# Output products with 17 weight columns, batch rows 16 partitions apart, and one output transfer of eight partitions in place of two of four

## The chip, the cores and the metric

One core of one Trainium2 chip. The time is device microseconds of one execution; lower is better. Each number of a run is the median of its executions. The execution's time is mostly 1.7 to 2.1 us longer than the span of its instructions, which the profile shows; both are given where it matters. Executions of one kernel on one chip mostly lie within 0.3%, so differences below that need several rounds, and their intervals are given.

## The reference, cut to what matters

One decoding step for two rows (B = 2): layernorm, attention with a window of 2048 of the cached keys and values for 16 key heads, its output product with `wo`, and beside it a squared-ReLU MLP, all added to the input.

```python
W = min(4096, max(256, Sk // 4))                 # 2048
k = k_cache[:, :, Sk - W:, :];  v = v_cache[:, :, Sk - W:, :]
o = softmax(q @ k.T * Dh ** -0.5) @ v             # per head
attention = o.reshape(B, 1, Hq * Dh) @ wo         # 4096 x 576
mlp = relu(xn @ w1 + b1) ** 2 @ w2 + b2           # 576 x 4608, 4608 x 576
return x + attention + mlp                        # (2, 1, 576), bf16
```

The core must read 53.6 MB and computes little on them.

## The kernel before

K and V of a unit (four heads of one batch row) are 2 MB each and go through one pool of six buffers of 16384 bytes in each partition; the weights of `wq`/`w1` and `wo` have pools of their own. All pools lie one behind the other in SBUF, after a pool `const` of small things, in this order:

```python
const  = ctx.enter_context(tc.tile_pool(name="const", bufs=1))
kvpool = ctx.enter_context(tc.tile_pool(name="kvpool", bufs=6))       # K, V, most of w2
ktpool = ctx.enter_context(tc.tile_pool(name="ktpool", bufs=6))       # K transposed: engines only
wbig   = ctx.enter_context(tc.tile_pool(name="wbig", bufs=NFULL // RW))   # wq, w1, the rest of w2
wrem   = ctx.enter_context(tc.tile_pool(name="wrem", bufs=2))
wopool = ctx.enter_context(tc.tile_pool(name="wopool", bufs=1))       # wo
...
def issue_kv(tiles, cache, u, name, parts=1):
    tl = kvpool.tile([P, UE], BF16, tag="kv", name=f"{name}_{u}")
    ...   # nc.sync.dma_start(out=tl[...], in_=v[...])
```

All products that end in the output have two weight columns (the two batch rows). Most go to `out_ps`, each with the two halves of the 576 columns in two column groups of TensorE; the last part of `w2`, which arrives last, goes to `tail_ps` in four groups of 144 columns:

```python
ones_b = const.tile([1, B], BF16, name="ones_b")
def out_acc(lhsT, rhs_of, start=False, stop=False, pin=False):
    for i in range(2):
        mm = nc.tensor.matmul(out_ps[32 * i:32 * i + B, :], lhsT=lhsT, rhs=rhs_of(i * OH, (i + 1) * OH), ...)
...
for i in range(4):
    cp = nc.scalar.copy if i % 2 else nc.vector.tensor_copy
    cp(out=part[32 * i:32 * i + B, :], in_=out_ps[32 * (i // 2):32 * (i // 2) + B, (i % 2) * OQ:(i % 2 + 1) * OQ])
for w in W2P[NG4 - 1:]:
    mlp_tail(*w[1:])                              # tail_ps, four groups
fin_sb = work.tile([RB, OQ], BF16, tag="fin", name="fin_sb")
nc.vector.tensor_tensor(out=fin_sb[:], in0=mlp["out"][0:RB, :], in1=part[:], op=ALU.add)
for b, eng in ((0, nc.sync), (1, nc.scalar)):
    eng.dma_start(out=out2d[b:b + 1, :].rearrange("o (q n) -> (o q) n", q=4), in_=fin_sb[b:RB:32, :])
```

So batch row b of quarter q lies in partition 32q + b, and each batch row leaves in a transfer of its own.

Of the kernel before, what the change touches and what calls it, by code (L numbers as in the profile page):

```python
# [8 lines left out]
F32 = mybir.dt.float32  # L9
BF16 = mybir.dt.bfloat16  # L10
ACT = mybir.ActivationFunctionType
ALU = mybir.AluOpType
# [4 lines left out]
def kernel(  # L17
# [14 lines left out]
    nc = tc.nc  # L32
    P = 128
    B, Sq, D = A_x.shape
# [27 lines left out]
    NG4 = 4  # L62
# [5 lines left out]
    FR = HW // P  # L68
# [7 lines left out]
    N3 = (NG4 - 1) * FR  # L76
    NFC = N3 + len(CX)
    RB = 32 * (NG4 - 1) + B
    OH = D // 2
    OQ = D // 4  # L80
    NP = NQ // 2
    WR = 2 * NC * Dh // P
# [3 lines left out]
    const = ctx.enter_context(tc.tile_pool(name="const", bufs=1))  # L86
    kvpool = ctx.enter_context(tc.tile_pool(name="kvpool", bufs=6))
    ktpool = ctx.enter_context(tc.tile_pool(name="ktpool", bufs=6))
    wbig = ctx.enter_context(tc.tile_pool(name="wbig", bufs=NFULL // RW))
    wrem = ctx.enter_context(tc.tile_pool(name="wrem", bufs=2))  # L90
    wopool = ctx.enter_context(tc.tile_pool(name="wopool", bufs=1))
    work = ctx.enter_context(tc.tile_pool(name="work", bufs=2))
    keep = ctx.enter_context(tc.tile_pool(name="keep", bufs=3))
    psum = ctx.enter_context(tc.tile_pool(name="psum", bufs=1, space=bass.MemoryType.PSUM))

    x2d = A_x.rearrange("b s d -> (b s) d")
    out2d = out.rearrange("b s d -> (b s) d")
# [74 lines left out]
    x_sb = const.tile([B, D], BF16, name="x_sb")  # L172
# [20 lines left out]
                                    scalar1=float(32 * q))  # L193
    ident = const.tile([P, P], BF16, name="ident")
    nc.vector.tensor_scalar(out=ident[:], in0=col_f[:], scalar1=row_f[:, 0:1], scalar2=None, op0=ALU.is_equal)
    ones_b = const.tile([1, B], BF16, name="ones_b")
    nc.vector.memset(ones_b[:], 1.0)

    half_d = D // 2
    stats = const.tile([B, 2, 6], F32, name="stats")  # L200
# [34 lines left out]
    with nc.allow_low_precision(reason="sums of one 1 and zeros"):  # L235
        nc.vector.tensor_reduce(out=rmask[:], in_=ident[:].rearrange("p (c r) -> p r c", r=WR), axis=AX.X, op=ALU.add)
        nc.vector.tensor_reduce(out=sel[:, MZ:MZ + DW], in_=ident[:].rearrange("p (c r) -> p c r", r=WR), axis=AX.X,
                                op=ALU.add)

    out_ps = psum.tile([32 + B, OH], F32, tag="out", name="out_ps")  # L240
    nc.vector.memset(out_ps[:], 0.0)

    def out_acc(lhsT, rhs_of, start=False, stop=False, pin=False):
        for i in range(2):
            mm = nc.tensor.matmul(out_ps[32 * i:32 * i + B, :], lhsT=lhsT, rhs=rhs_of(i * OH, (i + 1) * OH),  # L245
                                  start=start, stop=stop, skip_group_check=True)
            if pin:
                tc.keep_in_program_order(mm)
# [7 lines left out]
    def q_block(c):  # L256
# [6 lines left out]
        if c == KC - 1:  # L263
            qrow = const.tile([RB, QW], BF16, tag="row", name="qrow")
            nc.vector.tensor_copy(out=qrow[:, 0:QB], in_=q_ps[0][0:RB, :])  # L265
            nc.scalar.copy(out=qrow[:, QB:QW], in_=q_ps[1][0:RB, :])
            qT_ps = psum.tile([P, QH, P], BF16, tag="sc", bufs=2, name="qT_ps")
            for i in range(QH):
                nc.tensor.transpose(out=qT_ps[:, i, 0:RB], in_=qrow[:, i * Dh:(i + 1) * Dh],
                                    identity=ident[0:RB, 0:RB])  # L270
            qT_v = qT_ps[:].rearrange("p i (g s) -> p i g s", s=32)
# [68 lines left out]
            pT_tiles.pop(u)  # L340

    wo_state = {}

    def wo_sel(t):
        rr = work.tile([P, WR, 2 * NC * B], BF16, tag="rr", bufs=1, name=f"rr_{t}")
        for i in range(2):
            oG = oG_tiles.pop(2 * t + i)
            nc.vector.tensor_tensor(
                out=rr[:, :, i * NC * B:(i + 1) * NC * B],
                in0=oG[:].rearrange("p h b -> p (h b)").unsqueeze(1).to_broadcast([P, WR, NC * B]),  # L350
                in1=rmask[:].unsqueeze(2).to_broadcast([P, WR, NC * B]), op=ALU.mult)
        wps = psum.tile([P, WR, B], F32, tag="misc", bufs=2, name=f"wps_{t}")
        for h in range(2 * NC):
            nc.tensor.matmul(wps[:], lhsT=sel[:, MZ - h * DW:MZ - h * DW + P],
                             rhs=rr[:, :, h * B:(h + 1) * B], start=(h == 0), stop=(h == 2 * NC - 1))
        ws = work.tile([P, WR, B], BF16, tag="ws", name=f"ws_{t}")
        nc.vector.tensor_copy(out=ws[:], in_=wps[:])  # L357
        wo_state[t] = ws

    def wo_acc(tq):  # L360
        ws = wo_state.pop(tq)
        wo_sb = wo_tiles.pop(tq)
        for r in range(WR):
            out_acc(ws[:, r, :], lambda a, z: wo_sb[:, r, a:z])

    mlp = {}
# [15 lines left out]
    def mlp_h_end():  # L382
        hrow = const.tile([RB, HW], BF16, tag="row", name="hrow")
        for k in range(3):
            t1_t = work.tile([P, NJ, NC], F32, tag="sub", name=f"t1_{k}")
            t1 = t1_t[:].rearrange("p j c -> p (j c)")[0:RB, 0:HB]
            nc.scalar.activation(out=t1, in_=mlp["ps"][k][0:RB, :], func=ACT.Relu)
            nc.vector.tensor_tensor(out=hrow[:, k * HB:(k + 1) * HB], in0=t1, in1=t1, op=ALU.mult)
        hT_sb = const.tile([P, NFC, B], BF16, name="hT_sb")
        ha = psum.tile([P, FR, 96], BF16, tag="sc", bufs=2, name="ha_ps")  # L390
        hb = psum.tile([P, len(CX), B], BF16, tag="sc", bufs=2, name="hb_ps")
        ra = 32 * (NG4 - 2) + B
        for r in range(FR):
            nc.tensor.transpose(out=ha[:, r, 0:ra], in_=hrow[0:ra, r:HW:FR], identity=ident[0:ra, 0:ra])
        rb = 32 * (NG4 - 1)
        for i, (c0, st, m) in enumerate(CX):
            nc.tensor.transpose(out=hb[0:m, i, :], in_=hrow[rb:RB, c0:c0 + (m - 1) * st + 1:st],
                                identity=ident[rb:RB, rb:RB])
        ha_v = ha[:].rearrange("p r (g s) -> p g r s", s=32)
        for b in range(B):  # L400
            nc.vector.tensor_copy(out=hT_sb[:, 0:N3, b].rearrange("p (g r) -> p g r", r=FR), in_=ha_v[:, :, :, b])
        for i0, i1, m in ((0, FT, P), (FT, FT + XR, XP), (FT + XR, len(CX), XQ)):
            nc.vector.tensor_copy(out=hT_sb[0:m, N3 + i0:N3 + i1, :], in_=hb[0:m, i0:i1, :])
        mlp["h"] = hT_sb

    def mlp_o(g, r0, r1):
        w2_sb = w2_tiles.pop((g, r0))
        for r in range(r0, r1):
            o = (r - r0) * D
            out_acc(mlp["h"][:, g * FR + r, :], lambda a, z: w2_sb[:, o + a:o + z], stop=(g == NG4 - 2 and r == r1 - 1))  # L410

    part = const.tile([RB, OQ], F32, name="part")
    nc.gpsimd.memset(part[:], 0.0)

    def mlp_tail(r0, r1):
        w2_sb = w2_tiles.pop((NG4 - 1, r0))
        if r0 == 0:
            mlp["out"] = psum.tile([P, OQ], F32, tag="misc", bufs=2, name="tail_ps")
            nc.vector.memset(mlp["out"][:], 0.0)
        for r in range(r0, r1):  # L420
            o = (r - r0) * D
            for i in range(4):
                nc.tensor.matmul(mlp["out"][32 * i:32 * i + B, :], lhsT=mlp["h"][:, (NG4 - 1) * FR + r, :],
                                 rhs=w2_sb[:, o + i * OQ:o + (i + 1) * OQ], start=(r == 0), stop=(r == FT - 1),
                                 skip_group_check=True, tile_position=(0, 32 * i))

# [5 lines left out]
    def load_k(u):  # L432
        for f in issue_kv(k_tiles, A_k_cache, u, "k"):
            f()
        if u >= 3:
            issue_w2x()
# [31 lines left out]
    for g in range(NG):  # L468
# [7 lines left out]
                          in_=ident[0:NG4, 0:NG4].unsqueeze(2).to_broadcast([NG4, NG4, 32]))  # L476
# [1 line left out]
    nc.scalar.dma_start(out=b2_sb[:], in_=B_b2.rearrange("(o n) -> o n", o=1))  # L478
    step(1, {})
    load_k(4)  # L480
    out_acc(ident[:B, :B], lambda a, z: x_sb[:, a:z], start=True)
    out_acc(ones_b[:, :], lambda a, z: b2_sb[:, a:z])
    for u in range(2, NU - 1):
        step(u, {})
# [14 lines left out]
    for g in range(NG):  # L499
        pv(NU - 3, g)  # L500
    wo_sel(0)
    wo_acc(0)
    for c in range(KC):
        mlp_h_block(c)
    mlp_h_end()
    step(NU - 1, {}, with_pv=False)
    for g in range(NG):
        pv(NU - 2, g)
    mlp_x()
    for g in range(NG):  # L510
        pv(NU - 1, g)
    wo_sel(1)
    wo_acc(1)
    for w in W2P[:NG4 - 1]:
        mlp_o(*w)
    for i in range(4):
        cp = nc.scalar.copy if i % 2 else nc.vector.tensor_copy
        cp(out=part[32 * i:32 * i + B, :],  # L518
           in_=out_ps[32 * (i // 2):32 * (i // 2) + B, (i % 2) * OQ:(i % 2 + 1) * OQ])
    for w in W2P[NG4 - 1:]:  # L520
        mlp_tail(*w[1:])

    fin_sb = work.tile([RB, OQ], BF16, tag="fin", name="fin_sb")
    nc.vector.tensor_tensor(out=fin_sb[:], in0=mlp["out"][0:RB, :], in1=part[:], op=ALU.add)
    for b, eng in ((0, nc.sync), (1, nc.scalar)):
        eng.dma_start(out=out2d[b:b + 1, :].rearrange("o (q n) -> (o q) n", q=4), in_=fin_sb[b:RB:32, :])


# [28 lines left out]
```

## Time and profile before

| | before |
|---|---|
| time, median of 4 | 135.34 us (135.30 to 135.54) |
| span in the profile | 133.8 us |
| last weights landed | 130.25 us |
| `fin_sb` done | 131.01 us |
| from there to the end of the span | 2.78 us |

Three numbers add up to the span: when the last weights have landed, how long until the sum is formed, and how long the output and the closing take. The lines behind them are in the prediction. One more view became important afterwards, the window from 30 to 112 us, in which nothing but steady loading happens. In the view of a window, after the window and its length come the busy times of the engines with their counts, then the granted TensorE clock, the DMA share (the times of all packets over that of 16 engines; where just above 1, they overlap a little) and the GB/s.

```profile
30.00:112.00 82.00, 68.95 (x1420) 63.06 (x1421) 41.58 (x85) 32.74 (x38) 5.05 (x13) 0.77 1.01 427
```

The DMA engines are busy all the time and move 427 GB/s.

### The profile page before, as it was taken

Reading aid. Unit: us, or ns where it says so; the run is one execution under the profiler, and the core shown is the slowest. Engines: PE = TensorE matmul, PEld = TensorE weight load, DVE = VectorE, ACT = ScalarE, POOL = GpSimd, SP = SyncE. Lnnn points to the kernel's source line nnn. Section 1 sums busy time; section 2 is a strip of 40 time slices with the busy share of each in tenths; the row PEclk is TensorE's granted clock in tenths of the full one; section 3 lists DMA queues with packets and bytes.
Section 4 is the critical chain, followed back from the end, with each engine's and each line's share of the span. In section 5 each row is a group of like instructions: output and inputs, shape, how many; then the busy total and the mean of one; then the engine's idle time right before and its main releaser. Section 6 shows DMA issues by size and latency. Waiting matters only on the chain.

```text
span 133.8 us, 4142 instructions
## 1 busy us (share of the span) xinstructions
PE 99.9 (75%) x1890; PEld 84.9 (63%) x1890; DVE 57.3 (43%) x136; ACT 44.8 (33%) x53; POOL 6.8 (5%) x22
## 2 busy tenths in 40 slices
PE   1063796696998689997956996898956999869470
PEld 0052382585987589897946995886525998646240
DVE  7532040555458459466475256437123246420010
ACT  6714030546357326535534607331030541100010
POOL 1000000011011011011011011001100001100000
PEclk9999999959599955968996558687797579756985
DMA  4999999999999999999999999999999999999950
GB/s 113 421 432 422 439 421 431 421 436 426 427 426 436 422 420 436 421 436 421 436 421 438 416 435 424 435 429 424 414 436 431 431 429 433 408 427 423 407 196 1
DMA packets 4438, 53.87 MB, mean 403 GB/s; under 512 B 539, under 2 KB 686, under 8 KB 1202
## 3 DMA queue, kind: packets, MB, share of 16 engines
q1 hardware_dynamic: 4328, 53.32, 94.1%
q8 instruction: 14, 0.23, 0.6%
q10 hardware_dynamic: 94, 0.31, 0.6%
q14 instruction: 2, 0.02, 0.0%
HBM read 53.62 MB, written 0.00 MB: 401 GB/s over the span
## 4 chain that ended last, share of the span: by engine, by line
DMA 76%; PE 12%; DVE 5%; ACT 1%; issue 1%; POOL 1%; SPq 0%; DVEq 0%; ACTq 0%
DMA k<-in_A_k_cache_dram 43%; DMA w<-in_B_w_dram 20%; DMA wq<-in_A_wq_dram 9%; PE kT_ps L282 5%; DMA b_sb<-in_B_b_dram 4%; PE sc_ps L297 2%; PE q_ps L260 2%; PE oT_ps L334 2%; DVE m L303 1%; DVE sub L311 1%; DVE kT L287 1%; DVE l L316 1%; ACT kT L285 1%; POOL gmax L307 1%; DVE qrow L265 1%
## 5 line engine op out<-in xcount | busy, mean ns | idle before, releaser
L282 PE MATMUL kT_ps<-ident,k 128*128 128x128 bf16 x512 | 51.8, 274 | 4.1 <-DVE kT L287 2.4
L282 PEld LDWEIGHTS <-k 128*128 128x128 bf16 x512 | 42.5, 125 | 5.7 <-issue 2.4
L285 ACT COPY kT<-kT_ps 128x1024 bf16<-128x1024 bf16 x32 | 31.9, 1010 | 37.4 <-PE kT_ps L282 36.0
L287 DVE COPY kT<-kT_ps 128x1024 bf16<-128x1024 bf16 x32 | 21.5, 683 | 28.1 <-PE kT_ps L282 27.6
L297 PE MATMUL sc_ps<-qT_all,kT 128*128 128x8 bf16 x512 | 22.0, 169 | 7.2 <-ACT kT L285 4.0
L297 PEld LDWEIGHTS <-kT 128*128 128x128 bf16 x512 | 20.0, 102 | 9.2 <-ACT kT L285 4.8
L334 PE MATMUL oT_ps<-pT,v 128*128 128x8 bf16 x512 | 15.4, 167 | 1.5 <-issue 1.0
L334 PEld LDWEIGHTS <-v 128*128 128x128 bf16 x512 | 14.2, 98 | 2.7 <-issue 1.9
L314 ACT ACTIVATE pT<-sub 128x512 bf16<-128x512 f32 x8 | 5.0, 631 | 20.4 <-DVE sub L311 20.4
L316 DVE TENSOR_REDUCE l<-pT 128x8 f32<-128x512 bf16 x8 | 8.6, 1070 | 3.7 <-ACT pT L314 3.6
L303 DVE TENSOR_REDUCE m<-sc_ps 128x8 f32<-128x512 f32 x8 | 5.5, 692 | 5.4 <-PE sc_ps L297 5.4
L245 PE MATMUL out_ps<-wo,ws 128*2 128x288 bf16 x64 | 7.1, 408 | 0.9 <-DVE ws L357 0.9
L307 POOL PARTITION_ALL_REDUCE gmax<-m x8 | 3.0, 374 | 85.7 <-DVE m L305 85.7
L245 PEld LDWEIGHTS <-ws 128*2 128x2 bf16 x64 | 3.7, 115 | 4.0 <-DVE ws L357 1.2
L245 PEld LDWEIGHTS <-hT_sb 128*2 128x2 bf16 (+2 forms) x80 | 3.3, 82 | 4.4 <-issue 3.0
L245 PE MATMUL out_ps<-w,hT_sb 128*2 128x288 bf16 x54 | 3.8, 285 | 2.6 <-DMA w<-in_B_w_dram 2.6
L260 PE MATMUL q_ps<-wq,xnT 128*2 128x512 bf16 x32 | 3.5, 494 | 2.9 <-DMA wq<-in_A_wq_dram 2.9
L311 DVE TENSOR_TENSOR sub<-sc_ps,gm 128x512 f32<-128x512 f32 x8 | 5.5, 691 | 0.3
L518 ACT COPY part<-out_ps 2x144 f32<-2x144 f32 x2 | 0.5, 268 | 15.0 <-DVE part L518 14.9
L518 DVE COPY part<-out_ps 2x144 f32<-2x144 f32 x2 | 0.6, 298 | 10.1 <-PE out_ps L245 10.1
L318 POOL PARTITION_ALL_REDUCE lsum<-l x8 | 3.2, 399 | 23.2 <-DVE l L316 23.2
L260 PEld LDWEIGHTS <-xnT 128*2 128x2 bf16 x40 | 0.9, 86 | 4.3 <-issue 3.7
(75 smaller groups left out, 46.1 us busy)
## 6 DMA issues: line engine op xcount, KB each, us to landing
k<-in_A_k_cache_dram SPq DMA_DIRECT2D x8, 2048.0 KB, 12.4
v<-in_A_v_cache_dram SPq DMA_DIRECT2D x8, 2048.0 KB, 24.8
wo<-in_A_wo_dram SPq DMA_DIRECT2D x2, 2304.0 KB
w<-in_B_w_dram SPq DMA_DIRECT2D x2, 2304.0 KB, 32.2
wq<-in_A_wq_dram SPq DMA_DIRECT2D x2, 2048.0 KB, 17.1
w<-in_B_w_dram SPq DMA_DIRECT2D x3, 1296.0 KB, 27.4
w_rem<-in_B_w_dram SPq DMA_DIRECT2D x1, 576.0 KB
w<-in_B_w_dram SPq DMA_DIRECT2D x1, 576.0 KB
```

The source lines that it names most:

```text
L245: mm = nc.tensor.matmul(out_ps[32 * i:32 * i + B, :], lhsT=lhsT, rhs=rhs_of(i * OH, (i + 1) * OH), start=start, stop=stop, skip_group_chec ...
L260: nc.tensor.matmul(q_ps[k][32 * g:32 * g + B, :], lhsT=xnT[:, xc, :], rhs=rhs, start=(c == 0), stop=(c == KC - 1), skip_group_check=True, ...
L282: nc.tensor.transpose(out=kT_ps[:, i * P:(i + 1) * P], in_=k_sb[:, j * Dh:(j + 1) * Dh], identity=ident[:])
L285: nc.scalar.copy(out=kT[:], in_=kT_ps[:])
L287: nc.vector.tensor_copy(out=kT[:], in_=kT_ps[:])
L297: nc.tensor.matmul(sc_ps[:, g * JG + i, :], lhsT=kT[:, i * P:(i + 1) * P], rhs=qT_all[:, b, tq * NC:(tq + 1) * NC], start=True, stop=True)
L303: nc.vector.tensor_reduce(out=m1[:], in_=sc_ps[:].rearrange("p j c -> p c j"), axis=AX.X, op=ALU.max)
L307: nc.gpsimd.partition_all_reduce(gmax[:], m2[:], channels=P, reduce_op=ReduceOp.max)
L311: nc.vector.tensor_tensor(out=sub[:], in0=sc_ps[:], in1=gm2[:].unsqueeze(1).to_broadcast([P, NJ, NC]), op=ALU.subtract)
L314: nc.scalar.activation(out=pT[:], in_=sub[:], func=ACT.Exp, scale=scale)
L316: nc.vector.tensor_reduce(out=l1[:], in_=pT[:].rearrange("p j c -> p c j"), axis=AX.X, op=ALU.add)
L334: nc.tensor.matmul(oT_ps[:], lhsT=v_sb[:, j * Dh:(j + 1) * Dh], rhs=pT_tiles[u][:, j, :], start=(j == 0), stop=(j == NJ - 1))
```

## The change

The batch rows of a product are put 16 partitions apart. Then the eight pieces of the output lie in partitions 0, 16, 32, ... 112, one even step, and a single transfer can take them all. For that every stationary operand gets 17 columns, of which columns 0 and 16 hold the batch rows and the rest are zeros, cleared once at the start. To make room, the pool of the remainder weights goes from two buffers to one.

```diff
+    BS = 16
+    MB = BS * (B - 1) + 1                                   # 17
+    RM = 32 * (NG4 - 1) + MB                                # 113
-    wrem = ctx.enter_context(tc.tile_pool(name="wrem", bufs=2))
+    wrem = ctx.enter_context(tc.tile_pool(name="wrem", bufs=1))
-    ones_b = const.tile([1, B], BF16, name="ones_b")
-    nc.vector.memset(ones_b[:], 1.0)
+    ones_b = const.tile([1, MB], BF16, name="ones_b")
+    nc.vector.memset(ones_b[:], 0.0)
+    nc.vector.memset(ones_b[:, 0:MB:BS], 1.0)
+    sel_b = const.tile([B, MB], BF16, name="sel_b")
+    ...                                                     # ident's two columns, 16 apart
-            mm = nc.tensor.matmul(out_ps[32 * i:32 * i + B, :], lhsT=lhsT, ...
+            mm = nc.tensor.matmul(out_ps[32 * i:32 * i + MB, :], lhsT=lhsT, ...
+    for t in range(NP):
+        ws_bufs.append(const.tile([P, WR, MB], BF16, name=f"ws_{t}"))
+        nc.gpsimd.memset(ws_bufs[t][:], 0.0)
+    hT_sb = const.tile([P, NFC, MB], BF16, name="hT_sb")
+    nc.gpsimd.memset(hT_sb[:], 0.0)
-        nc.vector.tensor_copy(out=ws[:], in_=wps[:])
+        nc.vector.tensor_copy(out=ws[:, :, 0:MB:BS], in_=wps[:])
-        hT_sb = const.tile([P, NFC, B], BF16, name="hT_sb")
...                                                          # the same for hT_sb, part, tail_ps
-    for b, eng in ((0, nc.sync), (1, nc.scalar)):
-        eng.dma_start(out=out2d[b:b + 1, :].rearrange("o (q n) -> (o q) n", q=4), in_=fin_sb[b:RB:32, :])
+    nc.scalar.dma_start(out=out2d.rearrange("b (q n) -> q b n", q=4), in_=fin_sb[0:RM:BS, :])
```

More of the change, by code (lines that the diff above doesn't have):

```diff
@@ L195 @@
     nc.vector.tensor_scalar(out=ident[:], in0=col_f[:], scalar1=row_f[:, 0:1], scalar2=None, op0=ALU.is_equal)
-    ones_b = const.tile([1, B], BF16, name="ones_b")
-    nc.vector.memset(ones_b[:], 1.0)
+    ones_b = const.tile([1, MB], BF16, name="ones_b")
+    nc.vector.memset(ones_b[:], 0.0)
+    nc.vector.memset(ones_b[:, 0:MB:BS], 1.0)
+    sel_b = const.tile([B, MB], BF16, name="sel_b")
+    nc.vector.memset(sel_b[:], 0.0)
+    nc.vector.tensor_copy(out=sel_b[:, 0:MB:BS], in_=ident[0:B, 0:B])
     half_d = D // 2
@@ L238 @@
                                 op=ALU.add)
-    out_ps = psum.tile([32 + B, OH], F32, tag="out", name="out_ps")
+    out_ps = psum.tile([32 + MB, OH], F32, tag="out", name="out_ps")
     nc.vector.memset(out_ps[:], 0.0)
@@ L244, in out_acc @@
         for i in range(2):
-            mm = nc.tensor.matmul(out_ps[32 * i:32 * i + B, :], lhsT=lhsT, rhs=rhs_of(i * OH, (i + 1) * OH),
+            mm = nc.tensor.matmul(out_ps[32 * i:32 * i + MB, :], lhsT=lhsT, rhs=rhs_of(i * OH, (i + 1) * OH),
                                   start=start, stop=stop, skip_group_check=True)
@@ L342 @@
     wo_state = {}
+    ws_bufs = []
+    for t in range(NP):
[3 more added lines that the diff above has]
+    nc.gpsimd.memset(hT_sb[:], 0.0)
     def wo_sel(t):
@@ L355, in wo_sel @@
                              rhs=rr[:, :, h * B:(h + 1) * B], start=(h == 0), stop=(h == 2 * NC - 1))
-        ws = work.tile([P, WR, B], BF16, tag="ws", name=f"ws_{t}")
-        nc.vector.tensor_copy(out=ws[:], in_=wps[:])
+        ws = ws_bufs[t]
+        nc.vector.tensor_copy(out=ws[:, :, 0:MB:BS], in_=wps[:])
         wo_state[t] = ws
@@ L400, in mlp_h_end @@
         for b in range(B):
-            nc.vector.tensor_copy(out=hT_sb[:, 0:N3, b].rearrange("p (g r) -> p g r", r=FR), in_=ha_v[:, :, :, b])
+            nc.vector.tensor_copy(out=hT_sb[:, 0:N3, BS * b].rearrange("p (g r) -> p g r", r=FR), in_=ha_v[:, :, :, b])
         for i0, i1, m in ((0, FT, P), (FT, FT + XR, XP), (FT + XR, len(CX), XQ)):
-            nc.vector.tensor_copy(out=hT_sb[0:m, N3 + i0:N3 + i1, :], in_=hb[0:m, i0:i1, :])
+            nc.vector.tensor_copy(out=hT_sb[0:m, N3 + i0:N3 + i1, 0:MB:BS], in_=hb[0:m, i0:i1, :])
         mlp["h"] = hT_sb
@@ L410, in mlp_o @@
             out_acc(mlp["h"][:, g * FR + r, :], lambda a, z: w2_sb[:, o + a:o + z], stop=(g == NG4 - 2 and r == r1 - 1))
-    part = const.tile([RB, OQ], F32, name="part")
+    part = const.tile([RM, OQ], F32, name="part")
     nc.gpsimd.memset(part[:], 0.0)
@@ L422, in mlp_tail @@
             for i in range(4):
-                nc.tensor.matmul(mlp["out"][32 * i:32 * i + B, :], lhsT=mlp["h"][:, (NG4 - 1) * FR + r, :],
+                nc.tensor.matmul(mlp["out"][32 * i:32 * i + MB, :], lhsT=mlp["h"][:, (NG4 - 1) * FR + r, :],
                                  rhs=w2_sb[:, o + i * OQ:o + (i + 1) * OQ], start=(r == 0), stop=(r == FT - 1),
@@ L480 @@
     load_k(4)
-    out_acc(ident[:B, :B], lambda a, z: x_sb[:, a:z], start=True)
+    out_acc(sel_b[:], lambda a, z: x_sb[:, a:z], start=True)
     out_acc(ones_b[:, :], lambda a, z: b2_sb[:, a:z])
@@ L517 @@
         cp = nc.scalar.copy if i % 2 else nc.vector.tensor_copy
-        cp(out=part[32 * i:32 * i + B, :],
-           in_=out_ps[32 * (i // 2):32 * (i // 2) + B, (i % 2) * OQ:(i % 2 + 1) * OQ])
+        cp(out=part[32 * i:32 * i + MB, :],
+           in_=out_ps[32 * (i // 2):32 * (i // 2) + MB, (i % 2) * OQ:(i % 2 + 1) * OQ])
     for w in W2P[NG4 - 1:]:
         mlp_tail(*w[1:])
-    fin_sb = work.tile([RB, OQ], BF16, tag="fin", name="fin_sb")
-    nc.vector.tensor_tensor(out=fin_sb[:], in0=mlp["out"][0:RB, :], in1=part[:], op=ALU.add)
-    for b, eng in ((0, nc.sync), (1, nc.scalar)):
-        eng.dma_start(out=out2d[b:b + 1, :].rearrange("o (q n) -> (o q) n", q=4), in_=fin_sb[b:RB:32, :])
+    fin_sb = work.tile([RM, OQ], BF16, tag="fin", name="fin_sb")
+    nc.vector.tensor_tensor(out=fin_sb[:], in0=mlp["out"][0:RM, :], in1=part[:], op=ALU.add)
+    nc.scalar.dma_start(out=out2d.rearrange("b (q n) -> q b n", q=4), in_=fin_sb[0:RM:BS, :])
 _INS = ['A_x', 'A_k_cache', 'A_v_cache', 'A_wq', 'A_wo', 'B_x', 'B_w1', 'B_b1', 'B_w2', 'B_b2']
```

## The prediction

> **What bounds the kernel now.** I read the page first: the 40 slices, for which resource is never idle, and the table of queues.
>
> ```profile
> span 133.8 us, 4142 instructions
> DMA  4999999999999999999999999999999999999950
> GB/s 113 421 432 422 439 421 431 421 436 426 427 426 436 422 420 436 421 436 421 436 421 438 416 435 424 435 429 424 414 436 431 431 429 433 408 427 423 407 196 1
> q1 hardware_dynamic: 4328, 53.32, 94.1%
> ```
>
> From the second slice to the 38th the transfers run at 9 tenths or more and near 427 GB/s; no engine comes close. Neither the bytes nor the order of the loads changes, so 130 of the 133.8 us stay as they are unless the change makes a load start late. What can move is the stretch after the last weight byte. So I read the chain that ended last, in order of time, from 103 us on:
>
> ```profile
> 103.32 26.58 DMA w<-in_B_w_dram
> 129.89 0.04 issue
> 129.93 0.68 PE tail_ps L423 x9
> 130.61 0.03 issue
> 130.64 0.02 DVEq L524
> 130.66 0.04 issue
> 130.71 0.31 DVE fin_sb L524
> ```
>
> and then the timeline from 122 us, to see what of the tensor engine's work is beside transfers:
>
> ```profile
> 122.68 1.27 PE L245 MATMUL out_ps<-w,hT_sb 128*2 128x288 bf16 x18
> 124.74 1.27 PE L245 MATMUL out_ps<-w,hT_sb 128*2 128x288 bf16 x18 [0.79 <-DMA w<-in_B_w_dram]
> 127.84 1.27 PE L245 MATMUL out_ps<-w,hT_sb 128*2 128x288 bf16 x18 [1.83 <-DMA w<-in_B_w_dram]
> 129.14 0.63 DVE L518 COPY part<-out_ps 2x144 f32<-2x144 f32 x2 [10.08 <-PE out_ps L245]
> 129.23 1.35 PE L423 MATMUL tail_ps<-w,hT_sb 128*2 128x144 bf16 x28
> 129.53 0.56 ACT L518 COPY part<-out_ps 2x144 f32<-2x144 f32 x2 [14.93 <-DVE part L518]
> 130.71 0.31 DVE L524 TENSOR_TENSOR fin_sb<-tail_ps,part 98x144 bf16<-98x144 f32 x1 [0.94 <-PE tail_ps L423]
> 131.04 0.66 SPq L526 DMA_DIRECT2D out_dram<-fin_sb  x1
> 131.04 0.60 ACTq L526 DMA_DIRECT2D out_dram<-fin_sb  x1
> ```
>
> The tensor engine waits 0.79 and 1.83 us for weights in the last blocks, so it has slack there. The chain stops at fin_sb (131.01 us), yet the span ends at 133.80: the other 2.8 us are the output's transfer and the closing of the program. Two more views show those: the windows over the very end, and what the sync engine waits for after 129 us.
>
> ```profile
> 131.64:132.28 0.64, 0.00 (x0) 0.00 (x0) 0.00 (x0) 0.00 (x0) 0.00 (x0) 0.50 0.00 0
> 132.28:132.38 0.10, 0.00 (x0) 0.00 (x0) 0.00 (x0) 0.00 (x0) 0.00 (x0) 0.50 0.06 12
> 132.38:132.55 0.17, 0.00 (x0) 0.00 (x0) 0.00 (x0) 0.00 (x0) 0.00 (x0) 0.50 0.00 0
> 132.55:132.65 0.10, 0.00 (x0) 0.00 (x0) 0.00 (x0) 0.00 (x0) 0.00 (x0) 0.50 0.06 12
> 132.65:133.80 1.15, 0.00 (x0) 0.00 (x0) 0.00 (x0) 0.00 (x0) 0.00 (x0) 0.50 0.00 0
> ```
>
> ```profile
> SPq L552 <- DMA out_dram<-fin_sb: 1.0, 2, 0.8
> ```
>
> The last columns are DMA share and GB/s: two separate bursts, one per output transfer. In the trace's packet records the first burst (packets at 132.286 to 132.350) is on the scalar engine's queue, the second (132.558 to 132.618) on the sync engine's, although both instructions started within 4 ns of each other. Their semaphores complete at 132.693 and 132.961. The sync engine waits at the end twice: 0.8 us until the scalar engine's output has landed, then 0.27 us more until its own has. From 132.961 to the end is a closing of 133.795 - 132.961 = 0.834 us, nothing in which belongs to the kernel's lines.
>
> **What the Trainium skill says.** (1) "DMA: Bandwidth & Descriptors", section "Issuing engines are not separate DMA queues": transfers from either engine run on the same 16 DMA engines, and issuing from two saves only the issue time. Here two issuers don't even save that cleanly: the pair starts together and the second's packets are 0.27 us behind. (2) Same page, "Why a DMA increments its semaphore by 16 and not by 1": a transfer is spread over the largest number of engines up to 16 that divides the slowest dimension of both sides. Four rows now give 4; the trace agrees, with four 288-byte packets and four of 4 bytes on each queue. For the new transfer, slowest dimension 8 on one side and 4 on the other, this gives 4 engines with two rows each. (3) "TensorE: Matmul & The Clock Gate", section "LDWEIGHTS (loading the stationary operand)": the load time is columns / 1.2 in ns. From that page I estimate 17/1.2 - 2/1.2 = 12.5 ns more per load. The trace agrees only in direction: the 128x2 loads of the tail mostly show 79 ns, the 128x128 loads of V in the same stretch 100 ns, so 126 columns cost about 20 ns in these records and not 105; part of a record is fixed.
>
> **The change part by part.**
>
> Output transfer. Removed: the sync engine's issue (0.66 us) and its transfer, which landed last. Kept: the scalar engine's issue (0.60 us) and transfer, now eight rows. If it starts as the scalar engine's did, its packets begin at 132.286 and its four engines move two rows each. A 288-byte packet takes 16 to 18 ns in the records, so +0.02 us; landing at 132.693 + 0.02 = 132.71. The last landing moves from 132.961 to 132.71: **-0.25 us**. This is all on the path.
>
> Last tail chunk. The last 144 KB land at 130.252, the matmuls start at 130.294 and take 0.28; then 0.13 us to the addition. Only weight loads after that landing lie bare: four of 17 columns, in four column groups that start 3 ns apart. One to two loads' worth of the estimate in (3): **+0.02 us**.
>
> Other products. The last 54 matmuls before the tail come in pairs (two column groups) 118 to 122 ns apart, which is 288 moving columns at 2.4 columns per ns; the tail's groups of four are 120 ns apart, 144 columns at the granted clock of 0.5. Moving columns set both; a load starts about 118 ns ahead and fits behind a matmul even at 100 ns. Expected: 0. Were none hidden, 27 pairs in the three blocks, at two loads of 12.5 ns each, are 0.68 us, which mostly goes into the waits of 0.79 and 1.83 us above; between blocks of the tail the margin is only about 0.1 us.
>
> Copies and addition. part grows from 2 to 17 partitions, fin_sb from 98 to 113. The free size stays 144. In these records partitions do not count: a 34x288 memset takes 298 ns, a 128x144 one 178. **0**. The ws and hT_sb copies write the same elements at a stride of 17 columns instead of contiguously; ws takes 192 ns now, at 118.9 us, and whatever it takes longer goes into the waits for weights that follow. **0** at the end.
>
> Setup. GpSimd gets three clears. Its clear of 248 columns takes 305 ns, of 144 columns 219, thus about 0.83 ns per column above 0.1; two of 272 and one of 799 columns add about 0.33 + 0.33 + 0.76 = 1.4 us by about 2.6 us. GpSimd is first needed at 28.2 us. The vector engine gets three clears (60 ns each) and one small copy (0.2) before 8 us; it idles 1.28 us there for rstd, and the first K arrives only at 8.36. **0**.
>
> One buffer fewer for the remainder weights. w_rem's load is issued at 61.28 us; its buffer is now the one that wq_rem held, last read by matmuls at 23.0 to 23.7. Free 38 us before it is needed. **0**.
>
> Sum: -0.25 + 0.02 = **-0.23 us**: 135.31 - 0.23 = 135.08.
>
> **The rivals.**
> (A) The gap of 0.27 us is not one of order but of kind: the second transfer lags because descriptor generation takes one transfer after the other, and eight rows in one transfer then take as long as twice four. For it: the start-up pair of a sync load and the scalar load of x (issued 7 ns apart, first packets 2.152 and 1.670 us) also shows one trailing. Against it: issue times do not grow with rows (the bias load of 4 rows took 0.26 us, that of one row 0.23). It would eat the gain: 135.3.
> (B) The scalar engine alone starts sooner, since nobody contends: the x load's first packet came 0.94 us after its instruction's start, the output's 1.24. Up to 0.3 us more: 134.8. Against: that load reads memory and has two rows, so it is a weak comparison.
> (C) Weight loads of 17 columns are not hidden, and the tail's blocks, with margins of 0.1 us, push the end: at most seven groups of one to four loads, 7 x 12.5 to 28 x 12.5 ns = 0.09 to 0.35 us: 135.2 to 135.4. Against: spacing set by moving columns.
> (D) The program is ordered anew by its scheduler, since the residual's product now waits for a selector built from the identity, and a K or V load is issued late. For it: this product stands at 2.9 us in the trace though the source has it after the second unit. Against: loads are issued 12 to 25 us ahead of their landing. If it happened: +0.2 us or more.
>
> **Range and chances.** The main effect is 0.2% of the time. The three runs of before spread over 0.24 us, so chance alone moves a median by some 0.1. B and the main reading bound it below at about 134.8; A, C and a little of D above at about 135.4. Predicted 135.08 us, range 134.80 to 135.40. Over 2% either way means 2.7 us, more than anything above except a broken load schedule: chances 0.01 faster, 0.98 within 2%, 0.01 slower.
>
> **What would show each step right or wrong.** Right: one burst of eight 288-byte packets on the scalar queue, starting about 1.24 us after the issue starts, with four 4-byte packets; the sync engine's second wait of 0.27 us gone; the stretch from fin_sb's end to the span's end down from 2.78 us to about 2.53; tail groups still 120 ns apart and out_ps pairs still 118 to 122. A: the burst, or an issue of about 0.9 us, ends at about 132.6 as before. B: the first packet comes within 1 us of the issue's start. C: pairs 130 ns apart or more, or fin_sb starting later than 0.46 us after the last weights land. D: the last weights land later than 130.25 us. The prediction is wrong if the time lies outside the range, above all if the transfers' steady stretch changes.

## The result, and the profile after

The kernel after took **136.45 us** (median of 4, 136.35 to 136.65), the kernel before 135.34: 1.1 us longer, outside the predicted range of 134.80 to 135.40. Ratios here and below are of one kernel's fast runs to those of the kernel before in the same rounds, and not quite the ratios of the medians (1.0082 here): 1.0075, 95% interval 1.0052 to 1.0097. The kernel before is timed anew on each chip below (medians of 135.5 to 135.9), so only ratios are compared across chips.

The chain of waits of the kernel after, in order of time from 104 us on:

```profile
104.06 26.81 DMA w<-in_B_w_dram
130.87 0.04 issue
130.91 0.64 PE tail_ps L435 x12
131.54 0.03 issue
131.57 0.02 DVEq L536
131.59 0.04 issue
131.64 0.31 DVE fin_sb L536
```

The pieces are those of before, in the same order, but the chain of tail products and `fin_sb` stands 0.93 us later. With the landing times of the trace the difference of the spans splits so:

| | before | after | difference |
|---|---|---|---|
| last weights landed | 130.252 us | 131.180 us | +0.928 |
| from there to the start of `fin_sb` | 0.453 us | 0.458 us | +0.005 |
| `fin_sb` itself | 0.308 us | 0.306 us | -0.002 |
| from its end to the end of the span | 2.782 us | 2.627 us | -0.155 |
| span | 133.795 us | 134.571 us | +0.776 |

The output behaved nearly as predicted. The loss is in the loads, of which the diff changes not a line. The same window as above, from 30 to 112 us, in which nothing but steady loading happens, for the kernel after:

```profile
30.00:112.00 82.00, 69.89 (x1443) 62.70 (x1444) 41.70 (x86) 32.15 (x37) 5.03 (x13) 0.74 1.01 423
```

The DMA engines are just as busy, but move 423 GB/s and not 427: over 82 us this is 82 x 4/427 = 0.8 us, most of the 0.93. So it was no late load and no wait; the transfers themselves ran slower. The trace's packet records show how. They hold, for each packet, its size and its time. Before, of the 1623 packets of 16384 bytes (rows of K and V) that start between 30 and 112 us, 98.5% took 611 ns, to the nanosecond. After, 98% were longer by 1 to 20 ns: 55% took 614 ns, 20% took 621. The 18432-byte packets of `wo` and `w1` went from 686 to 689 and 696. By time, for the packets of 1152 bytes and more on the sync engine's queue:

| stretch | packets longer by 1 to 20 ns, before | after |
|---|---|---|
| 8 to 12 us | 0% | 21% |
| 12 to 20 us | 1% | 5% |
| 20 to 24 us | 0% | 33% |
| 24 to 112 us | 1% | 97% |
| 112 to 120 us | 0% | 67% |
| 120 us to the last weights | 1% | 36% |

Nothing in the diff speaks of K or `w1`. But the new tiles lie in `const`, ahead of all other pools. The program as built lists the addresses (no trace shows them): the first K buffer starts at byte 43520 of each partition before and at 46112 after, 2592 bytes further (32 for `ones_b`, 64 for `sel_b`, 1088 for the two `ws`, 1408 for `hT_sb`). 43520 is 85 x 512. 46112 is 32 past a multiple of 64, and of 256, and since the sizes of the buffers are multiples of 512, all load buffers behind it stand equally off. That is the theory that the experiments test.

### The profile page after: what moved, and what is told of

The parts are those of the page before. It is cut to its first block, busy times and chain, and to the rows that moved or that the text cites. A ratio compares the mean times of both kernels' runs of the same rounds, so it can differ in the third digit from the quotient of the medians.

```text
span 134.6 us, 4147 instructions
## 1 busy us (share of the span) xinstructions
PE 100.2 (74%) x1890; PEld 84.7 (63%) x1890; DVE 57.4 (43%) x139; ACT 44.6 (33%) x53; POOL 8.0 (6%) x25
## 4 chain that ended last, share of the span: by engine, by line
DMA 76%; PE 13%; DVE 5%; ACT 1%; issue 1%; POOL 1%; SPq 0%; DVEq 0%; ACTq 0%
DMA k<-in_A_k_cache_dram 44%; DMA w<-in_B_w_dram 20%; DMA wq<-in_A_wq_dram 9%; PE kT_ps L289 6%; DMA b_sb<-in_B_b_dram 3%; PE sc_ps L304 2%; PE q_ps L267 2%; PE oT_ps L341 2%; DVE m L310 1%; DVE sub L318 1%; DVE kT L294 1%; DVE l L323 1%; ACT kT L292 1%; POOL gmax L314 1%; DVE qrow L272 1%
## 5 line engine op out<-in xcount | busy, mean ns | idle before, releaser
L289 PE MATMUL kT_ps<-ident,k 128*128 128x128 bf16 x512 | 48.9, 263 | 6.9 <-DMA k<-in_A_k_cache_dram 5.0
L289 PEld LDWEIGHTS <-k 128*128 128x128 bf16 x512 | 39.8, 119 | 8.4 <-DMA k<-in_A_k_cache_dram 5.3
L252 PE MATMUL out_ps<-wo,ws 128*17 128x288 bf16 x64 | 8.0, 442 | 1.8 <-DMA wo<-in_A_wo_dram 1.1
L252 PEld LDWEIGHTS <-ws 128*17 128x17 bf16 x64 | 4.7, 133 | 4.3 <-issue 1.5
L252 PEld LDWEIGHTS <-hT_sb 128*17 128x17 bf16 (+2 forms) x80 | 4.3, 101 | 4.8 <-issue 3.4
L530 ACT COPY part<-out_ps 17x144 f32<-17x144 f32 x2 | 0.5, 268 | 16.8 <-DVE part L530 16.8
L252 PE MATMUL out_ps<-w,hT_sb 128*17 128x288 bf16 x54 | 3.8, 286 | 3.0 <-DMA w<-in_B_w_dram 3.0
L530 DVE COPY part<-out_ps 17x144 f32<-17x144 f32 x2 | 0.6, 300 | 11.8 <-PE out_ps L252 11.4
L267 PE MATMUL q_ps<-wq,xnT 128*2 128x512 bf16 x32 | 2.9, 499 | 2.3 <-DMA wq<-in_A_wq_dram 2.3
L401 DVE TENSOR_TENSOR hrow<-t 98x384 bf16<-98x384 f32 x3 | 1.6, 555 | 5.5 <-ACT t L400 5.3
```

Source lines behind the costliest of these rows:

```text
L252: mm = nc.tensor.matmul(out_ps[32 * i:32 * i + MB, :], lhsT=lhsT, rhs=rhs_of(i * OH, (i + 1) * OH), start=start, stop=stop, skip_group_che ...
L267: nc.tensor.matmul(q_ps[k][32 * g:32 * g + B, :], lhsT=xnT[:, xc, :], rhs=rhs, start=(c == 0), stop=(c == KC - 1), skip_group_check=True, ...
L289: nc.tensor.transpose(out=kT_ps[:, i * P:(i + 1) * P], in_=k_sb[:, j * Dh:(j + 1) * Dh], identity=ident[:])
```

## The experiments

**Theory 1**: where in SBUF a load's destination starts decides how long its packets take. **Theory 2**, the rival: the address is chance, and the 17 weight columns or the altered order of the first instructions slow the loads. A kernel needs only an unused stretch of bytes to tell them apart; in all that follows the order of instructions on each engine stays as in the kernel it is made from, except where it says otherwise.

### Moving the buffers, in both kernels

Each variant makes one small tile wider than is used. A tile takes a multiple of 32 bytes in each partition, hence the odd counts.

```diff
 # after + 32                                   after + 480: MB + 255
-    ones_b = const.tile([1, MB], BF16, name="ones_b")
+    ones_b = const.tile([1, MB + 31], BF16, name="ones_b")[:, 0:MB]
 # before + 32                                  before + 64, 128, 256, 512: B + 32, 64, 128, 256
-    ones_b = const.tile([1, B], BF16, name="ones_b")
+    ones_b = const.tile([1, B + 16], BF16, name="ones_b")[:, 0:B]
```

The kernel after, moved by 32 bytes:

> The kernel after, with one unused stretch of 32 bytes more in each partition, so that every buffer behind it starts at a multiple of 64 bytes again, as in the kernel before (in the kernel after, all large buffers start 32 bytes past a multiple of 64). Instructions and their order are the kernel after's. Theory 1 (the start address of the buffers stretches the load packets while the engines work): the 16384-byte packets take 611 ns again throughout (after: 614 and 621 from 24 us to 116 us), the last weights land near 130.25 us and the time is about 135.1 to 135.2 us, ratio to before 0.998 to 0.999. Theory 2 (17 weight columns, or the new order of instructions, cost it): 136.4 us as after, packets 614.

The kernel before, moved by 32 bytes:

> The kernel before, with one unused stretch of 32 bytes more, so that every buffer behind it starts 32 bytes past a multiple of 64. Nothing else is changed and the order of instructions is the same. Theory 1: packets 614 and 621 ns from about 24 us on, last weights at about 131.1 us, time 136.2 to 136.5 us, ratio 1.006 to 1.009. Theory 2: 135.3 us, packets 611.

The kernel before, moved by 64 bytes:

> The kernel before, with 64 bytes more: addresses move, but stay multiples of 64 (they are no longer multiples of 512). Theory 1 with 64 bytes as the unit: 135.3 us as before, packets 611. If a larger unit counts (128, 256 or 512 bytes): slower, some 135.8 to 136.5. Theory 2: 135.3.

The second run is the clear one: the kernel before, with 32 unused bytes and nothing else, ran at 1.0075 (1.0042 to 1.0108), the same ratio as the change. Theory 2 fell there. But my form of theory 1, with 64 bytes as the unit, fell too: the kernel after was still slow with its buffers at multiples of 64 (1.0053), and so was the kernel before moved by 64 (1.0054). A larger unit was needed, and the next four runs look for it.

The kernel after, moved by 480 bytes to multiples of 512:

> The kernel after with 480 unused bytes more in each partition, so that all buffers that large loads write start at a multiple of 512 bytes, as they do in the kernel before (there by chance: K's first buffer at 43520 = 85 x 512). Theory 1, now with 512 or 256 bytes as the unit: the 16384-byte packets take 611 ns throughout, the last weights land near 130.2 us, span about 133.6, ratio to before 0.998 to 0.999: the predicted gain of 0.2 us comes out. Theory 2 (17 weight columns or the order of instructions; the three moves of before slowed for another reason): 1.005 or more, packets of 613 and up.

The kernel before, moved by 128 bytes:

> The kernel before, buffers moved by 128 bytes: they start at 128 past a multiple of 512. If the unit is 128 bytes: as before, packets 611, ratio 1.000. If it is 256 or 512: packets 613 or so from 24 us on, ratio 1.004 to 1.007.

The kernel before, moved by 256 bytes:

> The kernel before, buffers moved by 256 bytes: 256 past a multiple of 512. If the unit is 256 bytes: as before, packets 611, ratio 1.000. If it is 512: packets 612 to 613, ratio 1.003 to 1.006.

The kernel before, moved by 512 bytes:

> The kernel before, buffers moved by 512 bytes: still at multiples of 512. Theory 1: as before, packets 611, ratio 0.999 to 1.001. If any move at all costs (some absolute address that before happens to hit, or a difference between the two programs in their first build): ratio 1.004 to 1.007.

| kernel | load buffers start past a multiple of 256 by | 16384-byte packets (most frequent) | longer by 1 to 20 ns | ratio to before (95%) |
|---|---|---|---|---|
| before | 0 | 611 | 1% | 1 |
| before + 512 | 0 | 611 | 1% | 0.9994 (0.9978 to 1.0010) |
| before + 256 | 0 | 611 | 1% | 0.9998 (0.9981 to 1.0015) |
| before + 128 | 128 | 611, 612, 613 | 68% | 1.0083 (1.0059 to 1.0107) |
| before + 64 | 64 | 613, 620 | 88% | 1.0054 (1.0023 to 1.0085) |
| before + 32 | 32 | 614, 621 | 98% | 1.0075 (1.0042 to 1.0108) |
| after | 32 | 614, 621 | 98% | 1.0075 (1.0052 to 1.0097) |
| after + 32 | 64 | 613, 620 | 93% | 1.0053 (1.0015 to 1.0091) |
| **after + 480** | 0 | 611 | 1% | **0.9973** (0.9960 to 0.9987) |

The packets are those that start between 30 and 112 us. The unit is **256 bytes**: off it, all three positions tried are slow, and on it, all are fast, in either kernel. Within the slow ones the ratios don't separate by position; the intervals overlap. The packets do: those at 32 are a nanosecond longer than those at 64, whichever kernel it is. The 1.0083 at 128, above what I had expected, holds two runs whose time was 2.5 and 2.8 us above their span; by the mean of the listed spans (to 0.1 us each) the four slow variants stand at 1.0064 to 1.0076, *before + 256* and *+ 512* at 1.0000 and 0.9999, *after + 480* at 0.9984.

With its buffers on the unit the kernel after takes 135.23 us against 135.59, and has the lowest ratio of all. Its steady window and its chain of waits:

```profile
30.00:112.00 82.00, 71.30 (x1462) 64.33 (x1464) 41.59 (x87) 31.95 (x37) 5.40 (x14) 0.75 1.01 428
```

```profile
108.03 22.07 DMA w<-in_B_w_dram
130.10 0.04 issue
130.14 0.27 PE tail_ps L435 x4
130.41 0.03 issue
130.44 0.02 DVEq L536
130.46 0.04 issue
130.50 0.31 DVE fin_sb L536
```

428 GB/s, and the last weights land at 130.10 us. Over all traces they land between 130.06 and 130.37 us where load buffers are on the unit or only those of the weights are off, between 130.99 and 131.36 where all of them are off, and at 130.74 with K and V alone off, of which below (the kernel with an eighth of the work is left out of this).

Two of the six runs of *after + 32* were 0.9 us slower than the other four (137.15 against 136.2 to 136.4), and the profile fell on one of them. It shows another cause, after the loads: the last weights landed at 131.16 us, as in the other kernels off the unit. Of the timeline of that run:

```profile
128.74 1.77 PE L252 MATMUL out_ps<-w,hT_sb 128*17 128x288 bf16 x14 [1.83 <-DMA w<-in_B_w_dram]
131.03 0.30 DVE L530 COPY part<-out_ps 17x144 f32<-17x144 f32 x1 [11.64 <-PE out_ps L252]
132.05 0.27 ACT L530 COPY part<-out_ps 17x144 f32<-17x144 f32 x1 [0.37 <-DVE part L530]
132.35 0.31 DVE L536 TENSOR_TENSOR fin_sb<-tail_ps,part 113x144 bf16<-113x144 f32 x1 [0.34 <-ACT part L530]
```

The last block of 18 products normally takes 1.27 us; here it took until about 131.0 (four of the products, in two pairs, stand between the tail's), and the granted clock over 128 to 131.2 us was 0.64 and not 0.82 as in the trace of the kernel after. That the lower clock made the block longer is likely, not tested. Then the four copies into `part`, each of which waits for the one before it, end at 132.3 and release `fin_sb`, 1.19 us after the last weights and not 0.46. Two of the six runs of the kernel with one output from the sync engine, below, were 0.9 us slower too, but no profile fell on them. Such runs widen the intervals; the packets of the one trace are like those of the others.

### Which buffers count

Here unused pools are put between the pools, so that some are 32 bytes off and the others are not:

```diff
 # K and V off by 32, all others by 64 (fourth run);  K and V alone: the second pad 480 bytes
+    pad0 = <tile of 32 bytes in a pool of its own>
     kvpool = ctx.enter_context(tc.tile_pool(name="kvpool", bufs=6))
+    pad1 = <tile of 32 bytes>
     ktpool = ctx.enter_context(tc.tile_pool(name="ktpool", bufs=6))
 # weights alone: 32 bytes ahead of wbig, 480 ahead of work
 # transposed K alone: 32 bytes ahead of ktpool, 480 ahead of wbig
```

Each pad is cleared in part by GpSimd at the start, two small instructions more.

> The kernel before with only the six buffers of K, V and most of w2 moved by 32 bytes; the buffers that the engines alone use (K transposed, scores, probabilities) and those of wq, wo and w1 stay at multiples of 64. Theory 1a (the destination of a load counts): K and V packets 614 and 621, the 18432-byte packets of wo and w1 686 as before; time about 135.9 to 136.2. Theory 1b (operands of the engines count, whichever buffer, for all loads then in flight): then K and V as operands of TensorE would stretch all packets, the 18432-byte ones to 689 too. If only the engines' own buffers count: 611 and 686, 135.3.

> The kernel before with only the buffers of wq, w1, wo and w2's last part moved by 32 bytes; K, V, the rest of w2 and all that the engines use alone stay at multiples of 512. If the destination of each load counts: the 18432-byte packets take 689 and 696 ns, the 16384-byte packets 611, also where both kinds are in flight together; ratio about 1.001 to 1.002. If the address of anything slows all loads: both kinds are stretched.

> The kernel before with only the buffers of transposed K, which the engines alone write and read, moved by 32 bytes. If only destinations of loads count: all packets 611 and 686, ratio 1.000. If engine operands off a multiple of 256 disturb the loads: packets of 614, ratio 1.002 to 1.007.

> The kernel before with only the six buffers of K, V and most of w2 32 bytes off, all others at multiples of 512. With the weights alone off, 1.0009. If the cost of the two sets simply adds up to that of all buffers (1.0075): about 1.005 to 1.007 here. If the stretching builds up only while all loads in flight are off (with the weights alone off it set in slowly): clearly less, 1.002 to 1.004. The 18432-byte packets of wo and w1, with aligned destinations: 686 if the packet's own destination counts, 688 and more if neighbours slow them.

| off the unit | 16384-byte packets longer | 18432-byte packets longer | ratio (95%) |
|---|---|---|---|
| K, V, w2 by 32; all others by 64 | 98%: 614, 621 | 96%: 688, 695 | 1.0062 (1.0031 to 1.0093) |
| weights alone, by 32 | 2% | 22%: 689, 696 | 1.0009 (0.9993 to 1.0024) |
| transposed K alone, by 32 | 1% | 0% | 0.9988 (0.9972 to 1.0005) |
| K, V, w2 alone, by 32 | 73%: 614, 621 | 10% | 1.0044 (1.0018 to 1.0071) |

Transposed K, which only engines touch, does not count. Of the first row (the fourth run made) I had expected 686 ns for the 18432-byte packets; its weights' buffers stood 64 past the unit, though, which I took for harmless then. So it failed as a separation but gave another sign: in one and the same trace packets to buffers at 32 show 614 and 621, and those to buffers at 64 show 688 and 695, each mostly the excess of its own position. So a packet's own destination counts.

But it does not decide alone. Packets with aligned destinations are longer too while others off the unit are in flight: with K and V alone off, 23 of the 33 aligned 18432-byte packets that start from 76 to 80 us, by 1 to 8 ns; with the weights alone off, 14 of the 23 aligned 16384-byte ones from 94 to 97 us, by 3 to 8 ns. The last expectation above, 686 ns or 688 and more, thus came out in between: 90% kept 686 ns. Nor are the packets off the unit longer at once. With the weights alone off, only a fifth were: of the 18432-byte packets, 83% of those that start from 82 to 85 us had their normal time, 55% from 91 to 94. With K and V alone off, some 13% of the packets are longer from 24 to 34 us and nearly all from 38 on; longer ones all but vanish between 80 and 100 us while aligned weights arrive, and come back from 104 us on. The costs of the two halves, 0.09% and 0.44%, add up to somewhat less than the 0.75% of all together, though the intervals are too wide to insist on that.

### Do the engines have a part in it?

The stretch in which packets are longer is the one in which TensorE, VectorE and ScalarE are busy. The kernel *before + 32* was given an eighth of the work on K and V. Its output is wrong, which doesn't matter for the time.

```diff
-        for i in range(JG):
+        for i in range(1):                       # transposes, scores, products with V
-            nc.scalar.copy(out=kT[:], in_=kT_ps[:])
+            nc.scalar.copy(out=kT[:, 0:P], in_=kT_ps[:, 0:P])
...                                               # softmax on every eighth column block
```

> The kernel before with every buffer 32 bytes off (as in the second experiment), and an eighth of the work on K and V: one transpose, one score and one product of eight, copies of 128 columns in place of 1024. The result is wrong on purpose. It asks why the packets are stretched only from about 24 to 116 us. If they need the engines' traffic in SBUF: 611 ns nearly everywhere. If it is among the DMA engines alone: 614 and 621 as with full work.

One profiled run, so no interval; the time was 136.45 us. (The output even passed the comparison with the reference, so that comparison does not see this part of the work; it does not make the kernel right.) From 30 to 112 us VectorE's busy time fell from 40.93 us (*before + 32*) to 19.10 and ScalarE's from 32.98 to 9.78; TensorE's matmuls went from 1382 to 327. And yet 97% of the 16384-byte packets were longer, at 614 and 621 ns, and all 18432-byte ones, setting in between 20 and 26 us as with full work. So the longer packets do not need most of TensorE's and ScalarE's work, nor half of VectorE's.

That their cost stays too is not shown. The steady window of *before + 32*, and then that of this kernel:

```profile
30.00:112.00 82.00, 67.65 (x1382) 60.93 (x1382) 40.93 (x84) 32.98 (x38) 5.05 (x13) 0.76 1.01 423
30.00:112.00 82.00, 29.54 (x327) 17.01 (x327) 19.10 (x88) 9.78 (x36) 5.34 (x14) 0.91 1.01 426
```

With light engines the transfers moved 426 GB/s, nearly the 427 of the kernel before, and the 16384-byte packets of the window took 617.8 ns on average, against 614.0 in the kernel before and 619.5 in *before + 32*. Of the last 128 packets of the weights the middle one started at 128.85 us; before it was 128.92, in *before + 32* 129.95. The time is as long as it is because a few of those 128 came late, the last at 130.60 us; a load of instructions of 1.03 us, which started at 126.03, is a possible reason, as in no other trace one starts between 122.6 and 130.1; that is argued and not tested. This kernel also loads fewer instructions (4 packets of 16384 bytes and not 14, some 0.4 us at 427 GB/s by my estimate), which hides a part of the cost. No run has light engines with the buffers on the unit. So whether the engines' work adds to the cost stays open, and so does whether it arises among the transfers alone.

### The output alone

The kernel after on the unit, with its output undone, and with its one transfer from the sync engine:

```diff
-    nc.scalar.dma_start(out=out2d.rearrange("b (q n) -> q b n", q=4), in_=fin_sb[0:RM:BS, :])
 # two outputs
+    for b, eng in ((0, nc.sync), (1, nc.scalar)):
+        eng.dma_start(out=out2d[b:b + 1, :].rearrange("o (q n) -> (o q) n", q=4), in_=fin_sb[BS * b:RM:32, :])
 # one output, sync engine
+    nc.sync.dma_start(out=out2d.rearrange("b (q n) -> q b n", q=4), in_=fin_sb[0:RM:BS, :])
```

> The kernel after with all buffers at multiples of 512 bytes (the previous experiment with 480 bytes), and its output undone: two transfers of four partitions from the sync and the scalar engine, as before. It tells what the single output transfer is worth by itself. From the traces so far: from the end of fin_sb to the end of the span 2.61 to 2.63 us with one transfer, 2.77 to 2.81 with two. So: 2.77 to 2.80 here, span about 133.6, and a ratio to before of 0.999 to 1.000, against 0.9973 with one transfer. If the gain of the aligned kernel comes from elsewhere: ratio about 0.997 also here.

> The kernel after with all buffers at multiples of 512 bytes and its one output transfer issued by the sync engine in place of the scalar engine. In the kernel before, the sync engine's output started its packets 0.27 us after the scalar engine's, though both were issued together. If that was order alone (descriptors are made for one transfer after the other): from the end of fin_sb to the end of the span 2.61 to 2.66 us, as with the scalar engine, ratio about 0.997. If it is the queue or the engine: 2.75 to 2.9 us, ratio about 0.999.

| kernel after, on the unit | from `fin_sb`'s end to the end of the span | ratio (95%) |
|---|---|---|
| one output, scalar engine | 2.613 us | 0.9973 (0.9960 to 0.9987) |
| two outputs | 2.856 us | 0.9989 (0.9975 to 1.0003) |
| one output, sync engine | 2.643 us | 0.9996 (0.9965 to 1.0027) |

The difference of the first two ratios is 0.16%, 0.22 us, and that of the traces 0.24 us; measured against the 2.77 to 2.81 us of the kernels with the layout of before, it is 0.16 to 0.20 us. The two ratios' intervals overlap, and they come from two chips, so it is the traces that show that the single output gains, and somewhat less than the prediction gave it. The sync engine's single output is as quick in the trace as the scalar engine's, 0.03 us apart. By this one trace the 0.27 us by which it had trailed came from being the second of two, not from its queue. The times of that run do not confirm it by themselves: four of its six runs were 135.36 to 135.54, two 136.3 to 136.4, as told above, and the interval holds everything.

## Why the prediction was wrong

Point by point, by its steps:

- **"Neither the bytes nor the order of the loads changes, so 130 of the 133.8 us stay as they are unless the change makes a load start late."** This is the step that failed. Bytes and order did stay (one small load of the scalar engine's was issued 3 us sooner, in *after + 480* too), and no load started late in a way that mattered, but the transfers ran slower, 423 GB/s in place of 427, because new small tiles moved the load buffers behind them off a multiple of 256 bytes. It cost 0.93 us of the span in the trace; 0 had been put down. Rival D expected late loads and its sign, last weights after 130.25 us, did appear, but its cause is ruled out: *before + 32* has the order of the kernel before and the same loss, *after + 480* the order of the kernel after and none. Of the same step, "no engine comes close" was read too lightly, as TensorE's row on the page reaches 9 tenths in 16 of the 40 slices; that the transfers bind holds all the same, as they are 76% of the chain that ended last.
- **One buffer fewer for the remainder weights, and the setup: 0.** As waits and work they were 0: GpSimd's clear of `hT_sb` took 0.77 us (worked out: 0.76) and the engines were ready for the first K. As bytes they were not: the three kinds of new tile in `const` are those 2592 bytes. I listed their instructions and not their addresses.
- **Output transfer, -0.25 us.** The mechanism was right and the size too large: -0.155 in the traces of before and after, -0.16 to -0.24 in the undone pair. Two terms were mis-sized. The packets started 1.262 us after the instruction's start and not 1.241, and the last landing was at 1.700 us and not 1.648 + 0.02, so -0.22 rather than -0.25 for the landing. And the closing grew from 0.834 to 0.896 us: the sync engine's last wait had been the one for its own output; now one more, of 0.062 us, follows that for the output.
- **One burst with four engines of two rows each**: eight packets of 288 bytes and four of 4 bytes, all on the scalar engine's queue. Right. What the sync engine waits for at the end, in the kernel after:

```profile
SPq L563 <- DMA out_dram<-fin_sb: 2.5, 1, 2.5
```

  It waits for the output once and not twice; the time is longer only because this engine has nothing of its own to issue meanwhile.
- **Last tail chunk, +0.02 us; other products, 0.** +0.005 us from the last weights to `fin_sb`. Weight loads of the tail took 95 ns (median) with 17 columns and 80 with two, close to the estimate of 12.5 ns more. Pairs of products still began 122 ns apart. Rival C did not happen.
- **Copies and addition, 0.** No effect on the end in these traces, but less slack than thought: the copies into `part` now take turns, VectorE waiting 0.39 us for ScalarE and the reverse, so the last ends at 131.32 us, 0.3 us before `fin_sb`. Where the clock was low in the last block, they became the bound.
- **Rival A** was half right: the lag is one of order. But eight rows in one transfer took about 0.05 us longer than four, not twice as long. **Rival B** did not happen.

The aligned kernel fits the sum of the other terms: 0.9973 of before, and the interval, 0.9960 to 0.9987, holds the 135.08/135.31 = 0.9983 predicted. Some of that is luck: of the 0.37 us by which its span is shorter in the trace, 0.17 come from the output and 0.15 from weights that landed earlier, and the landings of the traces on the unit alone spread over 0.3 us.

What is shown: the loss comes with load destinations off a multiple of 256 bytes, goes with it, needs no change in the program's work, and does not come from the buffers of transposed K, which only engines use; the longer packets, though not surely the loss, stay when half to three quarters of the engines' work is gone. What stays open is why the longer packets build up over ten microseconds or so and fade again. No run shows a reason. Open too is a part of the delay: the times of all packets of the sync engine's queue, over 16 engines, grew by 0.64 us of the 0.93. The trace narrows the rest: the last 128 packets of that queue start 0.81 us later on average and the last of them 0.86, so some 0.17 us of the rest lies between packets, and little in a different end of the single engines.

## What to carry to other kernels

In a kernel bound by its loads, look at where the load buffers start in SBUF after any change to what is allocated ahead of them: a small tile more in an early pool can move them all. Put buffers that loads fill at multiples of 256 bytes (here: a pad, or the large pools ahead of the small ones), and compare two kernels only with that held equal. If a change that "touches no load" moves the landing of the last load, compare the times of single packets first.

## What the Trainium skill lacked or had wrong

- "SBUF — State Buffer", section "Operand start alignment", treats the start address of an operand, a DMA's included, as a matter of what is legal, and says itself that its runs timed nothing. No page gives a cost of the start address of a load's destination. The runs: 1.0053 to 1.0083 of the time at 32, 64 and 128 bytes past a multiple of 256; 0.9998 and 0.9994 at multiples of 256 and 512.
- "DMA: Bandwidth & Descriptors", section "How a descriptor splits into AXI transactions", has the unit: pieces of 256 bytes, and extra beats of 32 bytes for a descriptor that does not start on one. I had not applied it, and it speaks of reads; the size does not fit either. My estimate by its rule for 16384 bytes is 513 beats in place of 512 at an offset of 32, 514 at 64 and 516 at 128, in every packet. Measured: 614 and 621 ns in place of 611 at 32, 613 and 620 at 64, and at 128 a third not longer at all; and from 12 to 20 us only 5% of the packets were longer at all.
- "DMA: Bandwidth & Descriptors", section "Latency and other measured facts", gives some 600 ns to the first byte of a transfer from the sync or scalar engine, without saying from when. For the output here the first packet began 1.26 us after the instruction's start, 0.64 us after its end (which agrees, if the end is meant), and the last semaphore followed the end of the last packet by 0.34 us. Of two such transfers issued together, no page says that the second trails, here by 0.27 us, and by 0.36 us in the run with two outputs on the unit.
